# Two positions per matmul in the k transforms, copies by one engine per PSUM tile, later batches reordered, w_out sums gated, loads per batch

## The chip, the core and the metric

The kernel runs on one core of a Trainium2 chip. The metric is the device time of one execution in microseconds (us), the median of several runs. A core has TensorE (matmuls; PE, and PEld for its weight loads), VectorE (DVE), ScalarE (ACT), GpSimd (POOL) and SyncE (SP); they run side by side, each through its own queue in order, and wait for each other through semaphores. DMA engines move data between DRAM and SBUF. Matmuls write PSUM; DVE and ACT read it out.

## What is computed

Block attention with sorted blocks, then a feed-forward layer with a squared ReLU. B = 4 batches, H = 8 heads, S = 768 positions in 8 blocks of 96, D = 64; d_model = 512, d_ff = 2048.

```
P = sort_net
for _ in range(5):                       # Sinkhorn: exp, rows to 1, columns to 1
    P = exp(P - max(P)); P = P / rowsum(P); P = P / colsum(P)
k_sorted[i] = sum_j P[i, j] k_block[j]   # likewise v
attn = softmax(q_block k_sorted^T / 8) v_sorted     # block by block
x = attn as [B*S, H*D]
out = (s * relu(x w_in)**2 + b) w_out
```

Within a block the order of the 96 positions of k and v does not matter, as long as both use the same one.

## The kernel before, in words

All inputs are cast to bf16 on load, by DMAs that POOL issues. A loop of small DVE and ACT instructions computes P (L188 to L208) while TensorE runs 46 dummy matmuls (`warm_up`, L176, L522). `block_rows` and `build_pd1` / `build_pd2` spread P into matrices `pd1` (batches 0 and 1, one batch per use) and `pd2` (batches 2 and 3 together).

**k.** `kb` holds k with (head, block) on partitions: batch 0 and 2 use rows 0 to 63, batch 1 and 3 rows 64 to 127. For each of the 96 positions in a block the k transform multiplies that position's `kb` slice with P. `k_piece1` (batches 0 and 1, L272) does two matmuls per position, one for even and one for odd heads, each into half of the partitions, 32 positions to a PSUM tile `tk`; one copy takes the tile to `ks`. `k_piece2` (batches 2 and 3 together, L283) does the same with 128 rows and 16 positions to a tile. So batch 0 takes 192 matmuls and 3 tiles, batch 1 the same, batches 2 and 3 together 192 matmuls and 6 tiles.

**v.** Batch 0's v is transformed directly into `VS[0]` (`v_piece0`, L292; 24 of the 64 columns go through `vt`, a copy that ACT makes in `v_perm`, L154). The other batches' v is transformed the other way round, written to DRAM (`dv`) and read back transposed (`v_read`, L336).

**Attention and feed-forward.** Time goes in eight half batches t = 0 to 7. Per t: four `s_piece` (scores and exp), four `p_piece` (times v, normalised into `X[t]`), one `t_piece` (transposed into `XT[t]`), `ffn1` (8 steps of 8 matmuls into `hps`, ACT's ReLU to `rt`, DVE's square to `gt`), `ffn2` (3 outputs tiles of 16 matmuls `ops`, DVE adds the bias, SP stores). Batch 0's preparation stands ahead of `ffn1(0)`, which goes in two halves of 192 columns. Everything later is cut into pieces that a `Queue` hands out between the matmuls of `ffn1` and `ffn2`: a queue of N pieces and n slots runs pieces until N * at // n are done at slot `at`. The order on each engine is the program's order.

**PSUM.** Two pools, whose buffers go round in the order in which tiles are asked for: `psa` (3 buffers of 2 banks: `hps`, `tk`, `tv`, `sc`, `tq`, `tr`, `bps`) and `psb` (2 buffers of 1 bank: `ops`, `pv`, `wp`, `pe`). Other pools: `rt` 3, `gt` 2, `vn` 6, `vs` 2, `qr` 2.

**Bias.** b times the column sums of w_out: POOL adds the 16 blocks of `wo` into `csum` (L557 to L559) as soon as w_out is there; `bias_piece` (L495), in `ffn2(0)`, multiplies it with ones and DVE makes `bias`. No `ops` tile is read out before that.

**Loads.** POOL issues, in order: v of batch 0, k of batch 0 in two parts, half of q, masks, w_in, the other half of q, v of batch 1, w_out, q and k of batch 1. v of batches 2 and 3 follows after `ffn1(1)`'s pieces, k of both and q of batch 2 after `ffn2(0)`.

Of the kernel before, what the change touches and what calls it, by code (L numbers as in the profile page):

```python
# [9 lines left out]
FP = mybir.dt.float32  # L10
# [8 lines left out]
def kernel(  # L19
# [12 lines left out]
    nc = tc.nc  # L32
# [239 lines left out]
    def k_piece1(b, c0, eng):  # L272

        pr = brows(b)[1]
        ps = psa.tile([128, CQ, 32], FP, tag="a", name="tk")
        for c in range(CQ):
            for e in range(2):
                nc.tensor.matmul(out=ps[e * 64:(e + 1) * 64, c, :], lhsT=kb[pr, c0 + c, :],  # L278
                                 rhs=pd1[pr, e], start=True, stop=True)
        g0 = (b % 2) * 32  # L280
        evac(ks[:, g0:g0 + 32, c0:c0 + CQ], ps.rearrange("p c g -> p g c"), eng)

    def k_piece2(c0, eng):  # L283

        ps = psa.tile([128, 16, 64], FP, tag="a", name="tk")
        for c in range(16):
            for e in range(2):
                nc.tensor.matmul(out=ps[e * 64:(e + 1) * 64, c, :], lhsT=kb[:, c0 + c, :],
                                 rhs=pd2[:, :, e], start=True, stop=True)
        evac(ks[:, :, c0:c0 + 16], ps.rearrange("p c g -> p g c"), eng)  # L290

    def v_piece0(d0, eng):  # L292

        ps = psa.tile([128, 16, 64], FP, tag="a", name="tv")
        rhs = pd1[0:64].rearrange("p e m i -> p (e m i)")
        for t in range(16):
            if d0 + t < NV:
                nc.tensor.matmul(out=ps[0:BLK, t, :], lhsT=vt[:, d0 + t, :], rhs=rhs,
                                 start=True, stop=True)
            else:  # L300
                nc.tensor.matmul(out=ps[:, t, :], lhsT=vb[0:64, :, d0 + t], rhs=rhs,  # L301
                                 start=True, stop=True)
        evac(VS[0][:, :, d0:d0 + 16], ps[0:BLK].rearrange("p t g -> p g t"), eng)

# [238 lines left out]
    def P(t, hp, *r):  # L543
# [21 lines left out]
    qu = Queue([lambda: (q_piece(1, 0, "s"), q_piece(1, 2, "v")), nothing,
                lambda: (k_piece1(1, 0, "v"), k_piece1(1, CQ, "s"), k_piece1(1, 2 * CQ, "v")),
                bias_piece, nothing, S2(2, 0), nothing, S2(2, 2), V2[0], V2[1], V2[2], V2[3],
                P2(2, 0), V2[4], P2(2, 2), seq(V2[5], lambda: v_read(2, nc.gpsimd)), S2(3, 0),
                T(2), P2(3, 0), S2(3, 2), nothing, P2(3, 2), nothing, T(3)], 24)
# [7 lines left out]
    def K2(i):
        return lambda: [k_piece2(16 * (i + j), "vsv"[j]) for j in range(3)]

    ffn1(2)  # L580
    ffn1(3, Queue([nothing, lambda: (q_piece(2, 0, "v"), q_piece(2, 2, "v")), nothing, K2(0),
                   nothing, nothing, K2(3), nothing], 8))
# [43 lines left out]
```

## Time and profile before

| | us |
|---|---|
| median of 3 runs | 264.79 (263.52 to 265.55) |
| profiled execution | 263.0 |
| its span, first to last instruction | 261.3 |
| DVE busy in the span | 124.5 (48%) |
| ACT busy in the span | 111.4 (43%) |
| POOL busy in the span | 36.2 (14%) |

A profile is one execution, taken by the hardware. The page gives busy time per engine; the span in 40 equal slices, where a digit is the busy share in tenths and PEclk the TensorE clock that was granted, in tenths of full speed; and the DMA queues. Other views group instructions by line and form, list busy times in chosen stretches, follow the chain of work that ended last back from the end, or list instructions in order of time. "L278" is line 278. "issue" stands where an engine waited for nothing that the profile shows.

### The profile page before, as it was taken

How to read it: one execution, taken by the hardware profiler on the slowest of the kernel's cores; microseconds unless marked ns; L12 is line 12 of the kernel's file. 1: busy time of each engine (PE TensorE's matmuls, PEld its weight loads, DVE VectorE, ACT ScalarE, POOL GpSimd, SP SyncE). 2: the span in 40 equal slices, each digit the busy share in tenths (PEclk: the TensorE clock that was granted, in tenths of full speed). 3: DMA queues.
4: the chain of work that ended last, by engine and by line, in shares of the span. 5: the costliest groups of instructions: out<-in, count | busy, mean ns of one | idle time of the engine just before them, and what ended most of it. 6: DMA issues, size and time to landing. Idle time of an engine off the chain costs nothing.

```text
span 261.3 us, 5765 instructions
## 1 busy us (share of the span) xinstructions
PE 239.3 (92%) x2536; PEld 145.9 (56%) x2556; DVE 124.5 (48%) x240; ACT 111.4 (43%) x139; POOL 36.2 (14%) x47
## 2 busy tenths in 40 slices
PE   8976889769994999999988999999999999999993
PEld 2466878754572455565654555556555555664441
DVE  5623849965651334634854525444446263442221
ACT  5542436554430466376454242466442427662000
POOL 7720039940002000520000000000000000000000
PEclk9975558999995999999999999999999999999998
DMA  4999999301598999399400111200011211000122
GB/s 52 201 209 209 211 207 214 76 0 28 96 220 105 204 243 304 112 180 134 77 3 3 49 74 41 83 0 3 0 43 40 80 43 41 3 0 20 63 80 82
DMA packets 20217, 25.02 MB, mean 96 GB/s; under 512 B 7456, under 2 KB 14368, under 8 KB 19744
## 3 DMA queue, kind: packets, MB, share of 16 engines
q0 software_dynamic: 8416, 15.21, 33.7%
q1 hardware_dynamic: 11776, 9.45, 13.0%
q8 instruction: 20, 0.33, 0.6%
q14 instruction: 5, 0.04, 0.0%
HBM read 29.63 MB, written 8.65 MB: 147 GB/s over the span
## 4 chain that ended last, share of the span: by engine, by line
PE 84%; DVE 9%; issue 3%; ACT 2%; DVEq 0%
PE ops L453 32%; PE hps L427 30%; PE wp L179 5%; DVE gt L432 4%; PE tk L278 3%; PE sc L353 3%; PE pv L380 3%; PE tr L408 2%; DVE x L385 1%; PE tv L301 1%; ACT rt L431 1%; PE tq L266 1%; PE tq L251 1%; PE tv L330 1%; DVE ks L235 1%
## 5 line engine op out<-in xcount | busy, mean ns | idle before, releaser
L427 PE MATMUL hps<-xt,wi 128*128 128x384 bf16 (+1 forms) x576 | 90.0, 313 | 6.3 <-DVE ks L235 2.0
L453 PE MATMUL ops<-wo,gt 128*128 128x512 bf16 x364 | 87.5, 381 | 1.7 <-issue 0.8
L427 PEld LDWEIGHTS <-wi 128*128 128x128 bf16 x576 | 54.9, 100 | 36.3 <-issue 8.3
L431 ACT ACTIVATE rt<-hps 128x768 bf16<-128x768 f32 (+1 forms) x72 | 53.2, 739 | 43.9 <-PE hps L427 42.9
L432 DVE TENSOR_TENSOR gt<-rt 128x768 bf16<-128x768 bf16 (+1 forms) x72 | 43.5, 611 | 49.8 <-ACT rt L431 49.7
L453 PEld LDWEIGHTS <-gt 128*128 128x128 bf16 x384 | 35.6, 98 | 39.7 <-issue 1.4
L356 ACT ACTIVATE at<-sc 96x768 bf16<-96x768 f32 x32 | 24.4, 802 | 29.9 <-PE sc L353 29.9
L444 DVE SCALAR_TENSOR_TENSOR ot<-ops,s_bc,bias 128x512 f32<-128x512 f32 x24 | 18.0, 749 | 39.7 <-PE ops L453 39.6
L385 DVE TENSOR_TENSOR x<-pv,rec 96x512 bf16<-96x512 f32 (+1 forms) x36 | 22.6, 628 | 1.2
L237 ACT COPY xt<-tr 128x1536 bf16<-128x1536 bf16 x7 | 10.1, 1438 | 23.9 <-PE tr L408 23.9
L559 POOL TENSOR_TENSOR csum<-csum,wo 128x512 f32<-128x512 f32 x14 | 16.2, 1155 | 1.1
L235 DVE CAST ks<-tk 128x1024 bf16<-128x1024 f32 x8 | 9.6, 1221 | 12.0 <-PE tk L278 12.0
L380 PEld LDWEIGHTS <-at 96*128 96x128 bf16 (+1 forms) x256 | 12.4, 105 | 4.8 <-ACT at L356 1.0
L278 PE MATMUL tk<-pd,kb 64*64 64x32 bf16 x384 | 8.1, 190 | 7.1 <-issue 6.2
L380 PE MATMUL pv<-vs,at 96*128 96x66 bf16 (+1 forms) x256 | 13.0, 200 | 1.3 <-DVE rec L384 0.9
L384 DVE RECIPROCAL rec<-pv 96x8 f32<-96x8 f32 (+1 forms) x36 | 6.9, 192 | 15.1 <-PE pv L380 15.1
L179 PE MATMUL wp<-zt 128*128 128x512 bf16 x46 | 12.7, 446 | 1.3 <-DVE warm L106 1.3
L278 PEld LDWEIGHTS <-kb 64*64 64x64 bf16 x384 | 7.8, 123 | 7.8 <-issue 7.7
L353 PEld LDWEIGHTS <-ks 64*96 64x96 bf16 x256 | 8.4, 127 | 5.7 <-issue 5.7
L353 PE MATMUL sc<-qt,ks 64*96 64x96 bf16 x256 | 10.9, 219 | 0.0
L237 ACT COPY qt<-tq 128x768 bf16<-128x768 bf16 (+1 forms) x6 | 5.9, 1014 | 10.9 <-PE tq L251 8.3
L179 PEld LDWEIGHTS <-zt 128*128 128x128 bf16 x46 | 5.0, 110 | 8.5 <-issue 3.5
(70 smaller groups left out, 126.3 us busy)
## 6 DMA issues: line engine op xcount, KB each, us to landing
out_dram<-ot SPq DMA_DIRECT2D x24, 256.0 KB, 2.0
qr<-in_q_dram POOLq DMA_DIRECT2D x3, 768.0 KB, 22.2
wi<-in_moe_w_in_dram POOLq DMA_DIRECT2D x2, 1024.0 KB, 16.9
wo<-in_moe_w_out_dram POOLq DMA_DIRECT2D x2, 1024.0 KB, 28.0
vb<-in_v_dram POOLq DMA_DIRECT2D x2, 768.0 KB, 15.4
vb<-in_v_dram POOLq DMA_DIRECT2D x1, 1536.0 KB, 10.8
kb<-in_k_dram POOLq DMA_DIRECT2D x1, 1536.0 KB, 13.5
dv<-vn SPq DMA_DIRECT2D x6, 256.0 KB, 6.7
```

The source lines that it names most:

```text
L179: nc.tensor.matmul(out=wp, lhsT=zt[:, 0:128], rhs=zt, start=True, stop=True)
L278: nc.tensor.matmul(out=ps[e * 64:(e + 1) * 64, c, :], lhsT=kb[pr, c0 + c, :], rhs=pd1[pr, e], start=True, stop=True)
L353: nc.tensor.matmul(out=sc[:, e, n * BLK:(n + 1) * BLK], lhsT=ks[pr, g0 + n, :], rhs=QT[b][pr, hp, q0:q0 + BLK], start=True, stop=True)
L356: nc.scalar.activation(out=at, in_=sc[:, :, 0:TG], func=AF.Exp, scale=scale)
L380: nc.tensor.matmul(out=pv[e][0:m, (n - n0) * VW:(n - n0 + 1) * VW], lhsT=atf[:, c0:c0 + m], rhs=VS[b][:, gi, :], start=True, stop=True)
L385: nc.vector.tensor_tensor(out=x[:, n0:n0 + nn, hp * 128:(hp + 1) * 128].rearrange("p n (e d) -> p e n d", e=2), in0=pvv[:, :, :, 0:D], in1 ...
L427: nc.tensor.matmul(out=hps[:, f, 0:nt], lhsT=wi_at(hp, f0 + f), rhs=xt[:, hp, c0:c0 + nt], start=(hp == 0), stop=(hp == NHP - 1))
L431: nc.scalar.activation(out=rt[:, :, 0:nt], in_=hps[:, :, 0:nt], func=AF.Relu)
L432: nc.vector.tensor_tensor(out=gt[:, f0:f0 + 2, c0:c0 + nt], in0=rt[:, :, 0:nt], in1=rt[:, :, 0:nt], op=ALU.mult)
L444: nc.vector.scalar_tensor_tensor(out=ot, in0=ops, scalar=s_bc, in1=bias, op0=ALU.mult, op1=ALU.add)
L453: nc.tensor.matmul(out=ops, lhsT=gt[:, f, m * 128:(m + 1) * 128], rhs=wo_at(f), start=(f == 0), stop=(f == NF - 1))
L559: nc.gpsimd.tensor_tensor(out=csum, in0=csum, in1=wo_at(f), op=ALU.add)
```

## The change

- **k transforms.** One `k_piece` for all batches. A matmul takes two neighbouring positions as its 128 weight columns and even and odd heads together as its columns: 48 matmuls for batch 0, 48 for batch 1, 48 for batches 2 and 3. The result has position parity on the partition halves where `ks` has head parity, so each tile is copied in four quarters of 64 partitions, all four by one engine. The quarters of one parity are `half(0)` and `half(1)`; for batches 2 and 3 they are queued as two pieces (`K2`). Batch 0 keeps the order of positions; for later batches even positions come first in `ks`, then odd ones, and `v_read` reads v in that order, in two DMAs.
- **Batch 0.** `vt` and `v_perm` are gone; all 64 columns of `v_piece0` come from `vb`. `q_half(0)` moves into the warm-up, which has 50 matmuls of 256 columns instead of 46 of 512. k is four tiles, copied by DVE, ACT, DVE, ACT. `build_pd2` moves behind `ffn1(0)`; two score pieces of t = 1 move ahead of it, two `V1` pieces behind it; `t_piece(1)` is copied by DVE instead of ACT.
- **w_out sums.** A one-element copy on POOL from the end of `X[1]` comes before them; they are split into 7 additions before and 8 after the load of v of batch 3.
- **Loads.** Half of q first, then k, v, the rest of q; v, k and q of batch 2 are issued ahead of `ffn1(0)`; batch 3's v and k are loaded by themselves.
- **Queues.** `ffn2(0)` and `ffn2(1)` have q and k of batch 1 in five slots instead of two; k of batches 2 and 3 is spread over `ffn1(2)` and `ffn1(3)` (15 pieces, 16 slots) instead of two lumps of three tiles in `ffn1(3)`.

```diff
-    load_v(*brows(0))
-    load_k(*brows(0), 2)
-    load_q(0, slice(0, 64))
+    load_q(0, slice(0, 64))
+    load_k(*brows(0))
+    load_v(*brows(0))
+    load_q(0, slice(64, 128))
...
-            wp = psb.tile([128, 512], FP, tag="b", name="wp")
+            wp = psb.tile([128, 256], FP, tag="b", name="wp")
...
+    def k_piece(b, c0, nc2, nb, eng):
...
+        pr = brows(b)[1] if nb == 1 else slice(0, 128)
+        rhs = (pd1[pr].rearrange("p e m i -> p (e m i)") if nb == 1
+               else pd2.rearrange("p b e m i -> p (b e m i)"))
+        if nc2 * nb > 8:
+            ps = psa.tile([128, nc2, nb * 64], FP, tag="a", name="tk")
+        else:
+            ps = psb.tile([128, nc2, nb * 64], FP, tag="b", name="tk")
+        for c in range(nc2):
+            nc.tensor.matmul(out=ps[:, c, :],
+                             lhsT=kb[pr, c0 + 2 * c:c0 + 2 * c + 2, :].rearrange("p c d -> p (c d)"),
+                             rhs=rhs, start=True, stop=True)
+        g0 = (b % 2) * 32
+
+        def half(cp):
+            if b == 0:
+                cs = slice(c0 + cp, c0 + 2 * nc2, 2)
+            else:
+                cs = slice(cp * (BLK // 2) + c0 // 2, cp * (BLK // 2) + c0 // 2 + nc2)
             for e in range(2):
...
+                evac(ks[e * 64:(e + 1) * 64, g0:g0 + nb * 32, cs].rearrange(
+                         "p (b g) c -> p b g c", b=nb),
+                     ps[cp * 64:(cp + 1) * 64].rearrange(
+                         "p c (b e g) -> p e b g c", b=nb, e=2)[:, e], eng)
+
+        half(0)
+        return lambda: half(1)
...
-    warm_up(46)
+    warm_up(38)
+    q_half(0, "s")
+    warm_up(12)
     build_pd1()
-    v_perm(16, NV)
-    for i, c0 in enumerate(range(0, BLK, CQ)):
-        k_piece1(0, c0, "vsv"[i])
-    q_half(0, "s")
-    v_piece0(0, "v")
-    v_piece0(16, "v")
+    k_piece(0, 0, 16, 1, "v")()
+    k_piece(0, 32, 16, 1, "s")()
+    k_piece(0, 64, 8, 1, "v")()
+    k_piece(0, 80, 8, 1, "s")()
+    v_piece0(0, 16, "v")
+    v_piece0(16, 16, "s")
+    v_piece0(32, 16, "v")
     s_piece(0, 0)
-    v_piece0(32, "v")
     s_piece(0, 1)
-    v_piece0(48, "v")
+    v_piece0(48, 16, "v")
     s_piece(0, 2)
     s_piece(0, 3)
-    build_pd2()
+    q_half(1, "s")
     for hp in range(NHP):
         p_piece(0, hp, 0, 2)
-    q_half(1, "s")
     t_piece(0, "v", 0, 2)
+    s_piece(1, 0)
+    s_piece(1, 1)
+
+    load_v(*brows(2))
+    load_k(*brows(2))
+    load_q(2)
...
+    gate = sk.tile([1, 1], BF)
+    nc.gpsimd.tensor_copy(out=gate, in_=X[1][0:1, HB - 1, d_model - 1:d_model])
...
+    csums(0, 8)
+    ffn1(1, Queue([V1(i) for i in range(2, 6)] + [lambda: v_read(1, nc.sync)] + [nothing] * 3, 8))
+    load_v(*brows(3))
+    csums(8, NF)
...
+    def K2(c0, eng):
+        return [lambda: rest.append(k_piece(2, c0, 8, 2, eng)), lambda: rest.pop()()]
+
+    pieces = [lambda: q_piece(2, 0, "v"), lambda: q_piece(2, 2, "v")]
+    for i in range(6):
+        pieces += K2(i * 16, "sv"[i % 2])
+    qu = Queue(pieces + [nothing], 16)
+    ffn1(2, qu)
+    ffn1(3, qu)
```

## Rows read from the trace of the kernel before

**Rows 1.** The page: TensorE's busy time, its granted clock in slices, its instruction queue.
```profile
PE 239.3 (92%) x2536; PEld 145.9 (56%) x2556; DVE 124.5 (48%) x240; ACT 111.4 (43%) x139; POOL 36.2 (14%) x47
...

...
q8 instruction: 20, 0.33, 0.6%
```

**Rows 2.** Busy times in stretches: engines, then granted clock, DMA share, GB/s.
```profile
15.26:36.52 21.26, 16.77 (x410) 15.84 (x410) 10.82 (x19) 6.99 (x9) 0.56 (x2) 0.54 1.16 210
36.52:58.15 21.63, 18.05 (x232) 16.13 (x232) 17.49 (x33) 11.87 (x22) 17.32 (x15) 0.90 0.65 113
...
71.19:111.26 40.07, 35.83 (x505) 20.96 (x510) 16.78 (x29) 16.78 (x18) 5.10 (x4) 0.91 0.95 196
111.26:139.87 28.61, 26.29 (x372) 17.07 (x371) 16.57 (x23) 15.55 (x19) 1.62 (x2) 1.00 0.62 89
```

**Rows 3.** The chain that ended last, in order of time: start us, us, what.
```profile
13.99 0.37 PE pe L220 x2
...
15.26 3.79 PE tk L278 x138
19.04 2.74 issue
...
59.61 0.33 PE tv L316 x2
...
75.51 2.70 PE tk L278 x164
78.21 3.48 issue
...
82.95 1.49 PE ops L453 x3
84.44 1.24 PE bps L497 x2
...
96.36 0.54 PE pv L380 x16
...
111.42 13.02 PE hps L427 x80
```

**Rows 4.** Instructions in order of time: the Sinkhorn loop's last one on DVE.
```profile
11.73 0.21 DVE L208 TENSOR_TENSOR sn<-sn,rrec 32x64 f32<-32x64 f32 x1
```

**Rows 5.** Instructions in order of time: POOL, held until earlier loads had landed.
```profile
10.47 0.92 POOL L161 DMA_DIRECT2D wo<-in_moe_w_out_dram  x1 [0.52 <-DMA vb<-in_v_dram]
...
16.67 0.54 POOL L90 DMA_DIRECT2D kb<-in_k_dram  x1 [1.39 <-DMA qr<-in_q_dram]
```

**Rows 6.** Instructions in order of time: v transforms of batch 0.
```profile
28.35 1.37 PE L301 MATMUL tv<-pd,vb 64*128 64x64 bf16 x14
```

**Rows 7.** Groups by line and form: busy us, mean ns of one, then idle before.
```profile
L431 ACT ACTIVATE rt<-hps 128x768 bf16<-128x768 f32 x56 | 45.4, 810 | 34.4 <-PE hps L427 34.4
L432 DVE TENSOR_TENSOR gt<-rt 128x768 bf16<-128x768 bf16 x56 | 31.2, 558 | 47.2 <-ACT rt L431 47.2
...
L235 DVE CAST ks<-tk 128x1024 bf16<-128x1024 f32 x8 | 9.6, 1221 | 12.0 <-PE tk L278 12.0
...
L235 DVE COPY qt<-tq 128x1536 bf16<-128x1536 bf16 x4 | 6.9, 1754 | 2.7 <-PE tq L266 2.7
...
L235 DVE CAST vn<-tv 128x512 bf16<-128x512 f32 x6 | 4.1, 683 | 0.0
L237 ACT CAST ks<-tk 128x1024 bf16<-128x1024 f32 x4 | 4.0, 1012 | 7.0 <-PE tk L278 6.4 <-PE tk L288 0.7
```

**Rows 8.** Instructions in order of time, ffn1(0): one addition on POOL, one square on DVE.
```profile
47.86 1.15 POOL L559 TENSOR_TENSOR csum<-csum,wo 128x512 f32<-128x512 f32 x1
47.92 1.31 DVE L432 TENSOR_TENSOR gt<-rt 128x384 bf16<-128x384 bf16 x1
```

**Rows 9.** Instructions in order of time, ffn1(3): TensorE after three tk tiles.
```profile
131.67 4.06 PE L427 MATMUL hps<-xt,wi 128*128 128x384 bf16 x24 [0.99 <-DVE ks L235]
```

More of the change, by code (lines that the diff above doesn't have):

```diff
@@ L75 @@
     vb = const.tile([128, 128, D], BF)
-    NV = 24
-    vt = sk.tile([64, NV, BLK], BF)
     qr = {}
@@ L101 @@
     nc.sync.dma_start(out=b_bc, in_=moe_b.to_broadcast([128, 1]))
-    zt = const.tile([128, 512], BF)
+    zt = const.tile([128, 256], BF)
     nc.vector.memset(zt, 0.0)
@@ L270, in q_piece @@
              ps[:, :, 0:S].rearrange("q a (t p) -> q a p t", t=TQ), eng)
[L272 to L276, printed above, removed]
-            for e in range(2):
[L278 to L303, printed above, removed]
+    def k_piece(b, c0, nc2, nb, eng):
[16 more added lines that the diff above has]
+                cs = slice(cp * (BLK // 2) + c0 // 2, cp * (BLK // 2) + c0 // 2 + nc2)
+            for e in range(2):
+                evac(ks[e * 64:(e + 1) * 64, g0:g0 + nb * 32, cs].rearrange(
[4 more added lines that the diff above has]
+        return lambda: half(1)
@@ new lines, in v_piece0 @@
+    def v_piece0(d0, n, eng):
+        if n > 8:
+            ps = psa.tile([128, n, 64], FP, tag="a", name="tv")
+        else:
+            ps = psb.tile([128, n, 64], FP, tag="b", name="tv")
+        for t in range(n):
+            nc.tensor.matmul(out=ps[:, t, :], lhsT=vb[0:64, :, d0 + t],
+                             rhs=pd1[0:64].rearrange("p e m i -> p (e m i)"),
+                             start=True, stop=True)
+        evac(VS[0][:, :, d0:d0 + n], ps[0:BLK].rearrange("p t g -> p g t"), eng)
@@ L339, in v_read @@
         src = dv[1] if b == 1 else dv[2][(b - 2) * 64:(b - 1) * 64]
-        eng.dma_start(out=VS[b][:, :, 0:D], in_=src.rearrange("g c d -> c g d"))
+        for cp in range(2):
+            eng.dma_start(out=VS[b][cp * (BLK // 2):(cp + 1) * (BLK // 2), :, 0:D],
+                          in_=src.rearrange("g (c two) d -> two c g d", two=2)[cp])
     XT, AT, X = {}, {}, {}
@@ L550, in V1 @@
         return lambda: v_piece1(i * 8, "v")
-    ffn1(0, Queue([P(0, 0, 2, 2), P(0, 1, 2, 2), P(0, 2, 2, 2), P(0, 3, 2, 2), SC(1, 0),
-                   lambda: t_piece(0, "v", 2, 2), SC(1, 1), SC(1, 2)], 8), 0, 2)
-    ffn1(0, Queue([SC(1, 3), P(1, 0), nothing, P(1, 1), P(1, 2), P(1, 3), nothing, T(1)], 8), 2, 2)
-    csum = const.tile([128, d_model], FP)
-    nc.gpsimd.tensor_tensor(out=csum, in0=wo_at(0), in1=wo_at(1), op=ALU.add)
-    for f in range(2, NF):
-        nc.gpsimd.tensor_tensor(out=csum, in0=csum, in1=wo_at(f), op=ALU.add)
@@ L561 @@
-    ffn1(1, Queue([V1(i) for i in range(6)] + [lambda: v_read(1, nc.sync), nothing], 8))
-    load_v(slice(128, 256), slice(0, 128))
-    V2 = [lambda c0=c0: v_piece2(c0, "s") for c0 in range(0, BLK, 16)]
[L565 to L569, printed above, removed]
+    ffn1(0, Queue([P(0, 0, 2, 2), P(0, 1, 2, 2), P(0, 2, 2, 2), P(0, 3, 2, 2), SC(1, 2),
+                   lambda: t_piece(0, "v", 2, 2), SC(1, 3), P(1, 0)], 8), 0, 2)
@@ new lines, with csums @@
+    ffn1(0, Queue([nothing, P(1, 1), nothing, P(1, 2), nothing, P(1, 3), nothing,
+                   lambda: t_piece(1, "v")], 8), 2, 2)
+    build_pd2()
+    V1(0)()
+    V1(1)()
+    csum = const.tile([128, d_model], FP)
+    gate = sk.tile([1, 1], BF)
+    nc.gpsimd.tensor_copy(out=gate, in_=X[1][0:1, HB - 1, d_model - 1:d_model])
+    def csums(f0, f1):
+        for f in range(f0, f1):
+            if f == 1:
+                nc.gpsimd.tensor_tensor(out=csum, in0=wo_at(0), in1=wo_at(1), op=ALU.add)
+            elif f > 1:
+                nc.gpsimd.tensor_tensor(out=csum, in0=csum, in1=wo_at(f), op=ALU.add)
@@ new lines @@
+    csums(0, 8)
+    ffn1(1, Queue([V1(i) for i in range(2, 6)] + [lambda: v_read(1, nc.sync)] + [nothing] * 3, 8))
+    load_v(*brows(3))
+    csums(8, NF)
+    V2 = [lambda c0=c0: v_piece2(c0, "s") for c0 in range(0, BLK, 16)]
+    qu = Queue([lambda: q_piece(1, 0, "s"), lambda: q_piece(1, 2, "v")]
+               + [lambda c0=c0: k_piece(1, c0, 16, 1, "vsv"[c0 // 32])() for c0 in range(0, BLK, 32)]
+               + [bias_piece, S2(2, 0), V2[0], S2(2, 2), V2[1], V2[2], V2[3],
+                  P2(2, 0), V2[4], P2(2, 2), seq(V2[5], lambda: v_read(2, nc.gpsimd)), S2(3, 0),
+                  T(2), P2(3, 0), S2(3, 2), nothing, P2(3, 2), nothing, T(3)], 24)
@@ L575 @@
     load_q(3)
[L577 to L582, printed above, removed]
+    rest = []
+    def K2(c0, eng):
[6 more added lines that the diff above has]
+    ffn1(3, qu)
     qu = Queue(attn(4) + attn(5), 24)
@@ L587 @@
     ffn1(5)
-    qu = Queue([lambda: (q_piece(3, 0, "s"), q_piece(3, 2, "v")), nothing]
+    qu = Queue([lambda: q_piece(3, 0, "s"), lambda: q_piece(3, 2, "v")]
                + attn(6) + attn(7), 24)
```

10 lines of the change are left out of this document (2 added, 8 removed).

## Prediction

> **What bounds the kernel now.** I read the share of the span per engine and the clock line first, then the busy times by stage, then the chain that ended last. TensorE is busy for 92% of the span [rows 1], so a change pays only where TensorE waits or runs slowly. [...] The stages [rows 2] are: before the first k transform (to 15.26 us), the rest of batch 0's preparation (15.26 to 36.52), ffn1(0) (36.52 to 58.15), ffn1(1) (to 71.19), ffn2(0) and (1) (71.19 to 111.26), ffn1(2) and (3) (to 139.87), and 121 us that the change hardly touches. The chain [rows 3] shows two naked waits, 2.74 us at 19.04 and 3.48 us at 78.21, both inside a run of tiny `tk` matmuls, named "issue": nothing in the profile held TensorE.
>
> What are they? Counting matmuls in program order, the first wait falls after the 223rd, the second after about the 990th. Each comes with one weight load, so 767 x 2 = 1534 instructions lie between them: six blocks of 256. The instruction queue [rows 1] moved 20 packets of 0.33 MB in all: 16 KB each, which for some 5,100 TensorE instructions is 256 a packet. So TensorE had used up a block and the next had not come. The previous block ends lie 128 matmuls earlier, at about 16.3 and 76.1 us by the spacing in [rows 3], so the next block came some 5.5 us after it each time, at a DMA share near 1 [rows 2]. 128 `tk` matmuls last 2.7 us; they outrun that.
>
> [...]
>
> **The change, part by part.** All at the profiled run's 263.0 us, span 261.3.
>
> *Start.* The Sinkhorn chain ends at 11.94 [rows 4], but warm-up holds TensorE until 13.99 [rows 3]. Now 50 warm-ups have half the columns, and `q_half(0)` stands among them. Warm-up columns until about 6.7 us run at half rate as now, so 25 of the 50 are done by then; the other 25 at 0.107 us and 48 transposes (some 0.8) end near 10.3, or near 11.2 where q is late: v's 0.79 MB released POOL at 10.47 and 1.97 MB at 16.67 [rows 5], so q's 0.39 MB, now first, should land by 8.5. k (1.18 MB in all) lands near 12.5 and v near 16.7, both in time. The step from `pe` to `pd1` stays 1.27 us, so `pd1` is ready at 13.25 instead of 15.26.
>
> *Batch 0, 13.25 to ffn1(0).* k: 48 matmuls for 192. Their shape isn't in the trace. Nearest are the v transforms (64x128 weights, 64 columns) at half clock, 14 in 1.37 us or about 0.09 each [rows 6], and, below, `pv` at full clock, 16 in 0.54 us, 0.034 [rows 3]. The copies get dearer: a quarter of a tile is 64 partitions by 512. No row has 64 partitions, but on DVE 512 elements take 0.68 us and 1024 take 1.22; on ACT 1024 take 1.01 and 768 take 0.81, so 512 about 0.6 [rows 7]. A tile copied once now costs four quarters: 2.7 us on DVE, 2.4 on ACT. Bounds: half the price (if 64 partitions were cheaper) and 1.22 (if a copy cost the same whatever its size). I take 0.68 and 0.6, since rows scale with elements.
> Walk at half clock: k tiles done 17.6; DVE copies the first until 17.4 and the third (256 elements a quarter) until 19.1, ACT the second until 18.4 and the fourth until 19.9. v tiles 1 to 3 end on TensorE at 19.0, 20.5, 21.9, two scores 23.0, the last v tile, which waits for a PSUM buffer, 24.6, two scores 25.7, `q_half(1)` 27.2, four `pv` with 0.6 us of DVE each 30.0, transposes 30.8, two scores of block 1, 31.9. The clock was still full 1.2 us after `pd1` before; the same again makes it 31.3. At full clock throughout the copies would set the pace: about 28. Gain 36.5 - 31.3 = **5.2**. `build_pd2` (1.5 us on this path before) moves behind ffn1(0), where the `xt` copy covers it.
>
> *ffn1(0), 21.63 us.* In it DVE sets the pace: a `gt` that starts beside a `csum` addition of POOL ends only after it, in 1.3 us [rows 8], where one of twice the elements takes 0.56 alone [rows 7]; so 0.35 is its own. The gate moves all 15 additions behind `X[1]`. Left is TensorE: 128 matmuls of 192 columns at half of 13.02/80 = 0.163 us [rows 3], 10.5; other pieces some 4.0; the first 3.9 us at half clock as before, +1.9; then `xt` copied by DVE (1.75, as `qt` [rows 7]). 18.1, gain **3.5**.
>
> *ffn1(1).* Two of six `V1` pieces leave (0.33 each [rows 3]): gain **0.6**. But the additions now run here. A `gt` of 768 elements (0.56 [rows 7]) waits for at most one addition, 1.15, which the `vn` copy (PSUM source) can use; with `vn` some 1.3 to 1.9 a step against 1.4 to 1.7 on TensorE. I take nothing (three `rt` buffers cover it); at worst 8 x 1.15 + 4 x 0.68 + 8 x 0.56 = 16.4 against 12.4, a loss of 4. POOL's queue: behind the gate wait stand 7 additions, `load_v(3)` (which waits for `V1`), 8 more; 15 x 1.23 = 18.5 us from 46 plus the load is 66, and the bias matmul comes at about 71. Nothing waits.
>
> *Loads.* v, k and q of batch 2 are issued earlier; DMA stays full until about 60 us instead of 48. The transfers of batch 1 are ahead of them in POOL's queue; SP's `dv` writes and `v_read(1)` (two DMAs instead of one, same bytes) share the engines, but `VS[1]` is wanted only 20 us later: zero.
>
> *ffn2(0), (1), 40.07 us.* k of batch 1 goes from 7.44 us (75.51 to 82.95, the wait in it) to 48 x 0.034 = 1.6 (bounds 1.6 to 4.3); the three `ops` and the bias after it ran at half clock, 1.49 + 1.24 [rows 3], and shrink by about 1.4. DVE has four quarters twice (5.4 us), `qt`, and then the bias; `S2(2,0)` waits about 0.6 for the last. Gain **6.7**. TensorE's blocks: 128 matmuls now take 9 us or more wherever DMA is full, against 5.5.
>
> *ffn1(2), (3), 28.61 us.* Now 15 pieces in 16 slots. A `tk` tile holds one of three psa buffers over two steps; buffers go round in order (after three `tk` the next `hps` waits for the first one's copy [rows 9]), so `hps` has two. With `hps` 1.30, `tk` 8 x 0.055 (128 columns, a third of 0.163, `hps` [rows 3]) = 0.45, `rt` 0.81 [rows 7]: an ACT tile runs `rt`, two quarters, `rt`, two quarters, 3.65 to 4.0 us from one `tk` to the next, a DVE tile 4.35, TensorE alone 3.05. Four steps and `q` 7.0, 0.35 more for the first tile, 22.7 for the rest: 30.05 to 30.2. **Loss 1.6**, bounds: 25 (only TensorE) and 33. [...]
>
> Sum: 5.2 + 3.5 + 0.6 + 6.7 - 1.6 = 14.4; 263.0 - 14.4 = 248.6. The profiled run lies 1.8 under the median of 264.79; I forecast **250**, between the two.
>
> **Rivals.**
> *A. The waits stay* at the k transforms, for a reason that isn't block size: 2.7 + 3.5 + 1.4 of half clock given back, near 257. For it: they sit at k both times. Against: the block count, and 192 of these matmuls at 129 to 138 us without a wait, when DMA was quiet. 0.10.
> *B. The additions bite again:* 4 us in ffn1(1), and if each also waits for a `gt` of 0.56, 8.4 us more on POOL, so the bias comes 4 late: 258. 0.10.
> *C. Full clock in the preparation* (-3.3) and `hps` in ffn1(2), (3) not held up (-3): near 244. For it: k keeps TensorE less starved. Against: the half clock came while TensorE was densely busy with small matmuls. 0.15.
> *D. Slower: a quarter costs what a tile cost* (1.22 and 1.01). Six tiles of batches 2 and 3: 3 x 4 x (0.54 + 0.4) = 11 us on that loop; 4.5 in the preparation, 4 in ffn2(0): 250 + 20 = 270. It decides from about 1.05 us a quarter. Against: [rows 7]. 0.05.
> My forecast, 246 to 254: 0.60.
>
> **Numbers.** 250 is the forecast's. Leaving out D, half of B's upper tail and C's far end, 243 to 258. A measurement of this kernel tells about 1% (2.6 us) from no change; under 262.1 lie the forecast, A, B and C but for their tails, 0.90; 0.05 within; 0.05 above 267.4.
>
> **What would show it.** `pd1` near 13.3; no "issue" wait over 1 us in any k transform; first `hps` near 31; quarters of 0.6 to 0.7 us; `gt` of ffn1(0) near 0.35 and stretched ones in ffn1(1); the stage of ffn2(0), (1) near 33.5; in ffn1(2), (3) `tk` waiting for `ks` copies, the stage near 30. I am wrong if a new block wait appears, if quarters cost over 0.9, or if bias waits for `csum`.

## The result, and the profile after

The changed kernel takes 249.4 us (median of 4 runs, 248.36 to 252.31); the kernel before, beside it, 265.17 (263.52 to 266.09). The ratio is 0.940, 95% interval 0.933 to 0.947: faster by nearly 16 us. 250.0 was forecast, in 243 to 258. The profiled execution took 249.47, its span is 247.8. Executions more than 1.5% above the fastest of their kernel are left out of every ratio.

First the clock line of the page of before, which the prediction reads, with its DMA line (tenths, 40 slices of 6.5 us, counted from 0; digit 5 of the clock line, in slices 3 to 5 and 12, is what the prediction calls the half clock):

```profile
PEclk9975558999995999999999999999999999999998
DMA  4999999301598999399400111200011211000122
```

The same from the page of after (slices of 6.2 us), with the busy times and the instruction queue:

```profile
PE 233.1 (94%) x2128; PEld 140.9 (57%) x2128; DVE 133.2 (54%) x260; ACT 116.3 (47%) x156; POOL 39.3 (16%) x51
...
PEclk9955579999999999999999999999999999999999
DMA  5999999999799929991001212000012120001122
...
q8 instruction: 16, 0.26, 0.5%
```

The second dip of the clock, slice 12, is gone. The hole in the DMA line is gone: before, the engines stood nearly still from 48 to 60 us (DMA share 0.02); after, they work through (1.07). The loads that fill it turn out to matter a great deal. Busy times by stage, columns as in [rows 2]; the stages are those of the prediction:

```profile
13.53:31.04 17.51, 14.68 (x233) 13.46 (x232) 11.23 (x20) 10.44 (x16) 2.31 (x4) 0.50 1.10 206
31.04:49.38 18.34, 17.02 (x224) 15.36 (x223) 12.98 (x37) 10.30 (x20) 2.99 (x5) 0.93 1.22 210
49.38:61.87 12.49, 12.24 (x74) 6.48 (x73) 11.36 (x14) 5.67 (x7) 10.46 (x10) 1.00 1.12 219
61.87:97.24 35.37, 34.29 (x368) 18.42 (x366) 21.93 (x36) 18.09 (x21) 11.39 (x10) 1.00 0.86 158
97.24:125.95 28.71, 26.30 (x228) 16.73 (x226) 18.13 (x28) 20.11 (x28) 1.63 (x2) 1.00 0.59 86
```

| stage | before | predicted | after |
|---|---|---|---|
| first k transform starts at | 15.26 | 13.25 | 13.53 |
| first `hps` starts at | 36.52 | 31.3 | 31.04 |
| ffn1(0) | 21.63 | 18.1 | 18.34 |
| ffn1(1) | 13.04 | 12.4 | 12.49 |
| ffn2(0), (1) | 40.07 | 33.4 | 35.37 |
| ffn1(2), (3) | 28.61 | 30.05 to 30.2 | 28.71 |

The chain of after has something that [rows 3] did not have: DMAs. Pieces in order of time, start, us, what:

```profile
13.25 0.23 DVE pd L511
13.53 1.88 PE tk L278 x32
...
60.91 8.34 DMA dv<-vn
...
69.39 0.34 SPq L345
...
69.78 12.35 DMA vs<-dv
...
82.17 0.71 PE pv L386 x16
```

The last write of batch 1's transformed v and its read back stand between 60.9 and 82.1, and the first `pv` of t = 2 waits for the read. In the list of instructions (start, us, then the idle time before and what ended it):

```profile
82.17 0.71 PE L386 MATMUL pv<-vs,at 96*128 96x66 bf16 x16 [1.03 <-DMA vs<-dv]
```

### The profile page after: what moved, and what is told of

The parts are those of the page before. It is cut to its first block, busy times and chain, and to the rows that moved or that the text cites. A ratio compares the mean times of both kernels' runs of the same rounds, so it can differ in the third digit from the quotient of the medians.

```text
span 247.8 us, 4978 instructions
## 1 busy us (share of the span) xinstructions
PE 233.1 (94%) x2128; PEld 140.9 (57%) x2128; DVE 133.2 (54%) x260; ACT 116.3 (47%) x156; POOL 39.3 (16%) x51
## 4 chain that ended last, share of the span: by engine, by line
PE 69%; DVE 12%; DMA 9%; ACT 6%; issue 1%; SPq 0%; DVEq 0%
PE ops L459 29%; PE hps L433 27%; DMA vs<-dv 5%; PE pv L386 4%; DVE gt L438 3%; DMA dv<-vn 3%; ACT rt L437 3%; PE sc L359 3%; PE tr L414 2%; ACT ks L230 2%; PE tv L304 2%; DVE ks L228 2%; DVE qt L228 1%; PE tk L278 1%; DMA sn<-in_sort_net_dram 1%
## 5 line engine op out<-in xcount | busy, mean ns | idle before, releaser
L459 PE MATMUL ops<-wo,gt 128*128 128x512 bf16 x384 | 90.5, 380 | 0.0
L230 ACT COPY xt<-tr 128x1536 bf16<-128x1536 bf16 x6 | 8.6, 1438 | 23.6 <-PE tr L414 23.6
L228 DVE CAST ks<-tk 64x512 bf16<-64x512 f32 (+1 forms) x28 | 18.5, 662 | 1.7 <-PE tk L278 1.3
L583 POOL TENSOR_TENSOR csum<-csum,wo 128x512 f32<-128x512 f32 x14 | 17.6, 1255 | 1.0
L230 ACT CAST ks<-tk 64x512 bf16<-64x512 f32 (+1 forms) x24 | 13.9, 580 | 7.2 <-PE tk L278 6.9
L172 PE MATMUL wp<-zt 128*128 128x256 bf16 x50 | 9.6, 321 | 1.1 <-DVE warm L104 1.1
L278 PE MATMUL tk<-pd,kb 64*128 64x64 bf16 (+1 forms) x144 | 8.3, 216 | 0.9 <-DVE pd L511 0.9
L278 PEld LDWEIGHTS <-kb 64*128 64x128 bf16 (+1 forms) x144 | 7.4, 106 | 3.0 <-issue 2.2
L228 DVE COPY qt<-tq 128x1536 bf16<-128x1536 bf16 x4 | 7.0, 1754 | 3.5 <-PE tq L259 3.5
## 6 DMA issues: line engine op xcount, KB each, us to landing
wo<-in_moe_w_out_dram POOLq DMA_DIRECT2D x2, 1024.0 KB, 30.2
```

The costliest lines, as they stand in the source:

```text
L278: nc.tensor.matmul(out=ps[:, c, :], lhsT=kb[pr, c0 + 2 * c:c0 + 2 * c + 2, :].rearrange("p c d -> p (c d)"), rhs=rhs, start=True, stop=True)
L459: nc.tensor.matmul(out=ops, lhsT=gt[:, f, m * 128:(m + 1) * 128], rhs=wo_at(f), start=(f == 0), stop=(f == NF - 1))
```

## Experiments

**The two waits belong to a count of instructions.** `e1_shift`, the kernel before with its warm-up matmuls twice as many and half as wide:

```diff
-            wp = psb.tile([128, 512], FP, tag="b", name="wp")
+            wp = psb.tile([128, 256], FP, tag="b", name="wp")
...
-    warm_up(46)
+    warm_up(92)
```

> The kernel before with 92 warm-up matmuls of 256 columns instead of 46 of 512: the same warm-up time, 46 matmuls more ahead of everything. Blocks of instructions (the prediction's reading): the waits sit at a count of TensorE matmuls (223 and about 990), so they come 46 matmuls earlier in the k transforms: after about 129 of batch 0's 192 instead of 175, after about 118 of batch 1's instead of 164. The block ahead ends at the first k matmul, so the first wait is about 2.7 us again (block due some 5.5 us after that end); for batch 1 the end falls in the ops ahead of k, so the second shrinks to some 2.0. Rival (something in the k transforms themselves, a tile, a copy or a load): both waits stay after the 175th and the 164th. The time stays within 2 us of the kernel before by either.

TensorE, instructions in order of time:

```profile
18.48 2.20 PE L278 MATMUL tk<-pd,kb 64*64 64x32 bf16 x129 [0.90 <-DVE pd L505]
23.65 1.52 PE L278 MATMUL tk<-pd,kb 64*64 64x32 bf16 x50 [2.98 <-issue]
...
80.17 2.04 PE L278 MATMUL tk<-pd,kb 64*64 64x32 bf16 x118
84.23 1.94 PE L278 MATMUL tk<-pd,kb 64*64 64x32 bf16 x66 [2.02 <-issue]
```

Against [rows 3] the first wait moved from the 175th matmul of the k transforms to the 129th, by the 46 matmuls put in ahead of it, and the second from the 164th to the 118th. Nothing else in the code of the transforms had changed. So the waits stand at a fixed place in the instruction stream, and the count of the prediction holds. That a block of 256 instructions ends there is its estimate, from that count and from the 20 packets of 0.33 MB [rows 1]; no trace shows a block arrive. The time, 272.31 us in a single run, misses the expectation of at most 2 us of change: the longer warm-up alone delayed the start by 3.2 us, and what made up the rest stays open.

Why the next block would come late is not shown either. In the tiny matmuls right ahead of the two waits of before (16.30 to 19.04 and 75.50 to 78.20 us) the DMA share was 1.12 and 1.01, ahead of the one of `e11_start` below (72.8 to 75.5) 1.02. In the first wait of before it was 1.25, but 0.28 in the second, columns as in [rows 2]:

```profile
78.20:81.70 3.50, 0.02 (x4) 0.01 (x2) 0.00 (x0) 0.49 (x1) 0.00 (x0) 0.51 0.28 66
```

So busy DMA engines alone do not explain it. The waits took 2.0 to 3.6 us each (2.74 and 3.48 before, 2.98 and 2.02 here, 3.57 in `e11_start`), and 1.55 us in `e2_oldk` below.

`e11_start`, the kernel before with the new start alone:

```diff
+    load_q(0, slice(0, 64))
+    load_k(*brows(0))
     load_v(*brows(0))
-    load_k(*brows(0), 2)
-    load_q(0, slice(0, 64))
+    load_q(0, slice(64, 128))
...
-    warm_up(46)
+    warm_up(38)
+    q_half(0, "s")
+    warm_up(12)
...
-    v_perm(16, NV)
```

> The kernel before with the new start alone: half of q first, then k, v, the rest of q; the warm-up of 50 matmuls of 256 columns with q_half(0) in it; v transformed from vb without ACT's copies. Old k transforms. My theory: k starts about 1.7 earlier (13.5); 52 more matmuls and transposes stand ahead of k, so the block end that fell at the 175th k matmul falls at about the 122nd, with the end before it in the transposes, 3 us before k starts: batch 0's wait shrinks from 2.74 to 0.5 or less; batch 1's stays at 3 to 3.5, 4 matmuls earlier (at about the 160th of 192). q_half (0.8) leaves the path behind k. 258.5 to 261. Rival (the wait belongs to k's matmuls, not to a block end): waits stay, 262 to 263.5.

260.64 us, ratio 0.985 (0.975 to 0.996).

```profile
13.54 5.30 PE L277 MATMUL tk<-pd,kb 64*64 64x32 bf16 x192 [0.90 <-DVE pd L500]
...
72.80 2.71 PE L277 MATMUL tk<-pd,kb 64*64 64x32 bf16 x160
79.07 1.04 PE L277 MATMUL tk<-pd,kb 64*64 64x32 bf16 x32 [3.57 <-issue]
```

Batch 0's wait is gone without any change of its transform; by the count the earlier block end now falls ahead of the k transforms. Batch 1's moved to the 160th, as foretold. The start is worth about 4 us (1 to 7 by the interval).

**Each part of the change undone alone.** `e2_oldk`, the changed kernel with the old k transforms for all batches (and the natural order with one read, which they imply):

```diff
-    k_piece(0, 0, 16, 1, "v")()
...
+    for i, c0 in enumerate(range(0, BLK, CQ)):
+        k_piece1(0, c0, "vsv"[i])
...
-        return [lambda: rest.append(k_piece(2, c0, 8, 2, eng)), lambda: rest.pop()()]
+        return [lambda: k_piece2(c0, eng), nothing]
```

> The changed kernel with the k transforms of before: four times as many matmuls, one copy per tile, positions in their natural order and v read back in one DMA per batch; all else as changed. Blocks of instructions: the block end falls on batch 0's 123rd k matmul, but the block before it ended near 11 us, so the next one is there by about 16.7: a wait of 0 to 1 us. In ffn2(0) a block end falls early in the third tile, 3.7 us after the one before it: a wait near 2 us. Together with 192 for 48 matmuls (some 1.5 us in the preparation, 1.5 in ffn2(0), 0.5 in ffn1(2) and (3)) the time rises by 4 to 5 us to about 254. Rival (the waits went because of the load order and the other rearrangements): no wait over 0.5 us, the time rises by 2 us at most, or falls where the copies were the limit.

250.75 us, ratio 0.949 (0.942 to 0.956): 1.2 us behind the changed kernel by the times, 2.4 by the ratios, whose intervals overlap; 4 to 5 were expected. The only trace is of an execution of 255.82 us, so its row shows where the wait falls, not what it costs:

```profile
75.30 1.25 PE L271 MATMUL tk<-pd,kb 64*64 64x32 bf16 x40 [1.55 <-issue]
```

It falls after 24 matmuls of the third tile, as the count says. The miss is in what the transforms are worth: with all the rest of the change in place, little. Why so little is not shown.

`e3_nogate`, the changed kernel without the gate:

```diff
-    gate = sk.tile([1, 1], BF)
-    nc.gpsimd.tensor_copy(out=gate, in_=X[1][0:1, HB - 1, d_model - 1:d_model])
```

> The changed kernel without the gate: the additions start as soon as w_out has landed, near 38 us, beside ffn1(0). If the gate is worth what the prediction says (3.5 us less in ffn1(0), nothing lost behind it): squares of ffn1(0) stretch to 1.1 to 1.3 us again, ffn1(0) takes 2.5 to 3.5 us longer, and the whole 2 to 3 us (252). Rival (the stretch is only moved from ffn1(0) to ffn1(1), where it costs as much, through the copies of V1 and the read of v behind them): ffn1(1) and the wait for VS[1] give it back, and the whole stays within 0.7 us.

249.29 us, 0.945 (0.941 to 0.950): not to be told from the changed kernel, as the rival has it. Seven additions ran from 36.9 to 45.4, ffn1(0) became 19.8 us long instead of 18.3, and three `hps` waited 0.46 to 0.64 us for DVE. Then ffn1(1) was quicker (12.2), the read of `VS[1]` was issued 1.8 us earlier, and the wait of 1.03 was gone. What ffn1(0) loses (1.5) is given back by the read's path (1.0), by ffn1(1) (0.3) and by a start 0.5 us earlier in this execution.

`e5_oneread`, the changed kernel with batch 1 in the natural order and one read:

```diff
-            if b == 0:
+            if b < 2:
                 cs = slice(c0 + cp, c0 + 2 * nc2, 2)
...
+        if b == 1:
+            eng.dma_start(out=VS[b][:, :, 0:D], in_=src.rearrange("g c d -> c g d"))
+            return
```

> The changed kernel with batch 1 in the natural order of positions, so that VS[1] is read by one DMA instead of two halves. In the changed kernel the read took 12.35 us from its issue, before 8.2, and TensorE waited 1.0 us for it. If the split makes the read slow: about 8 us, no wait for VS[1], the whole 1 us shorter (248.4). Rival (the read is late and slow because of what else the DMA engines carry then, the loads of batches 2 and 3): still 11 to 12 us, the wait stays within 0.3 of 1.0, the same time.

249.79 us, 0.948 (0.941 to 0.955): the same. The single read, issued at 68.28, took 13.5 us, so the split is not what made it slow. The `pv` of t = 2 starts without a wait at 82.17. But in the profiled execution the clock rose later, ffn1(0) took 19.3 us, and ffn1(2) begins at 97.24 as in the changed kernel; a gain of 1 us could not be shown.

**Each part alone, on the kernel before.** `e10_gateonly`, gate and split of the additions:

```diff
-    for f in range(2, NF):
-        nc.gpsimd.tensor_tensor(out=csum, in0=csum, in1=wo_at(f), op=ALU.add)
...
+    nc.gpsimd.tensor_copy(out=gate, in_=X[1][0:1, HB - 1, d_model - 1:d_model])
...
+    csums(0, 8)
...
     load_v(slice(128, 256), slice(0, 128))
+    csums(8, NF)
```

> The kernel before with the w_out sums gated behind X[1] and split around the load of v, nothing else. The prediction's step: gt in ffn1(0) at 0.35 instead of 1.31, so ffn1(0) about 2 to 3 shorter; six V1 steps in ffn1(1) then meet the additions, gt there 1.4 to 1.9, ffn1(1) 0 to 1 longer: 261 to 262.5. Rival (as undoing the gate in the changed kernel showed no change): 264 to 265, what ffn1(0) gains comes back in ffn1(1) or in a later bias.

262.02 us, 0.992 (0.988 to 0.996), as expected: ffn1(0) 19.5 us instead of 21.6, ffn1(1) 13.0 as before.

`e9_newk`, the new k transforms alone:

```diff
-        k_piece1(0, c0, "vsv"[i])
+        k_piece(0, c0, 16, 1, "vsv"[i])()
...
-        return lambda: [k_piece2(16 * (i + j), "vsv"[j]) for j in range(3)]
+        return lambda: [k_piece(2, 16 * (i + j), 8, 2, "vsv"[j])() for j in range(3)]
```

> The kernel before with the new k transforms alone: two positions per matmul, four quarter copies per tile by one engine, in the old order, same lumps, natural order of positions. My theory (TensorE outran its instruction blocks in the 192 tiny matmuls): block ends stay at the 95th, 223rd, ... matmul; with 144 matmuls fewer in batch 0 the 223rd lies in the v transforms, which are slower, and batch 1's k falls between two ends, so both waits of 2.74 and 3.48 us are gone. Batch 0: first hps 2 to 3.5 earlier (two tiles of four quarters on DVE take back some). ffn2(0), (1): 5 to 6.5 shorter. ffn1(3): lumps of three tiles whose copies cost 2.7 and 2.4 us instead of 1.2 and 1.0, 2 to 4 longer. In all 255 to 259. Rival (the k transform is worth what undoing it in the changed kernel cost, 1 to 1.5 us): 262 to 264, and waits stay at k.

267.36 us, 1.010 (1.005 to 1.015): slower than before, against both theories. Both waits in the k transforms are gone, the first `hps` starts at 33.90 (before 36.52), and batch 1's k transforms end 8 us earlier than before. Then the chain has:

```profile
68.68 10.18 DMA dv<-vn
...
79.01 16.51 DMA vs<-dv
```

and, on TensorE and on POOL in order of time:

```profile
95.57 1.11 PE L389 MATMUL pv<-vs,at 96*128 96x66 bf16 x16 [6.30 <-DMA vs<-dv]
...
75.12 0.54 POOL L90 DMA_DIRECT2D kb<-in_k_dram  x1 [7.52 <-PE tk L285]
```

The same rows in the kernel before, with the line of its DMA view that gives the time to landing (us, last):

```profile
82.92 0.54 POOL L90 DMA_DIRECT2D kb<-in_k_dram  x1 [13.12 <-PE tk L278]
...
80.43 0.34 SPq L340 DMA_DIRECT2D vs<-dv  x1
...
96.20 0.70 PE L380 MATMUL pv<-vs,at 96*128 96x66 bf16 x16
...
vs<-dv SPq DMA_DIRECT2D x1, 768.0 KB, 8.2
```

Before, the read of `VS[1]` (0.77 MB) is issued at 80.4 and lands 8.2 us later; k of batches 2 and 3 (1.5 MB) is issued 2.5 us after it, because it overwrites `kb` and waits for batch 1's transforms; q of batch 2 (0.75 MB) follows right behind. Faster transforms release both loads from 75.1 on, ahead of the read, and the read takes 16.5 us. The `pv` that needs it starts at 95.57 instead of 96.20: of 8 us on TensorE, 0.6 are left. And the wait leaves something behind it, columns as in [rows 2]:

```profile
95.57:99.60 4.03, 4.00 (x23) 2.06 (x25) 1.69 (x4) 0.32 (x1) 0.00 (x0) 0.53 1.00 381
```

The granted clock was 0.53 in these 4 us, where it was 1.00 before (96.20 to 100.20); the first four `ops` of them took 1.90 us instead of 1.03, and from the first `pv` to the second it takes 4.48 us instead of 2.69. So ffn1(2) begins 1.15 us later than before, and ffn1(3), where three tiles of four quarter copies come in one lump, adds 2.3.

`e12_newkloads`, the same with the loads per batch:

```diff
+    load_v(*brows(2))
+    load_k(*brows(2))
+    load_q(2)
...
-    load_v(slice(128, 256), slice(0, 128))
+    load_v(*brows(3))
...
-    load_k(slice(128, 256), slice(0, 128))
-    load_q(2)
+    load_k(*brows(3))
```

> The kernel before with the new k transforms and the loads per batch: v, k and q of batch 2 ahead of ffn1(0), v and k of batch 3 by themselves; all else as before. Theory: the 6.3 us wait for VS[1] that the new k transforms alone ran into shrinks to 0 to 2, since only half as many bytes stand ahead of the dv writes and beside the read: 258 to 261, so two parts of which one alone loses bring 3 to 6 us together. Rival (the read is late for another reason, as the DMA writes of dv themselves): still 264 to 268.

259.47 us, 0.981 (0.973 to 0.988), in the range of the theory. The read is issued at 72.65, takes 11.4 us, and `pv` starts without a wait at 86.85; ffn1(2) begins at 101.9, 9.4 us earlier than before. In ffn1(3) the lumps remain:

```profile
123.50 5.74 PE L436 MATMUL hps<-xt,wi 128*128 128x384 bf16 x24 [2.30 <-ACT ks L237]
...
133.03 1.46 PE L436 MATMUL hps<-xt,wi 128*128 128x384 bf16 x8 [2.29 <-ACT ks L237]
```

They waited 0.99 before [rows 9]; from ffn1(2)'s start to the second of these rows it takes 31.1 us instead of 27.1. In `e9_newk`, with the same two waits and the clock at 1.00, it takes 29.4; here the clock was 0.68 from 124.0 to 129.4, behind the first wait, and the 24 `hps` there took 5.74 us instead of 4.06. So in lumps the new transforms lose 2.3 us or more; spreading the pieces over sixteen slots should take that back, but no run has the spread alone.

**Loads late, in the changed kernel.** `e8_lateloads` moves only the loads of batch 2:

```diff
-    load_v(*brows(2))
-    load_k(*brows(2))
-    load_q(2)
...
+    load_v(*brows(2))
     load_v(*brows(3))
...
     ffn2(0, qu)
+    load_k(*brows(2))
     load_k(*brows(3))
+    load_q(2)
```

> The changed kernel with batch 2's loads late: v of batch 2 with that of batch 3 behind V1, k and q of batch 2 with k of batch 3 behind the k transforms of batch 1. Theory (from the trace of the new k transforms alone, where the k load followed the earlier k transforms at 75.1 us and the read of VS[1], issued at 79.0, took 16.5 us to land instead of 8.2): the early loads per batch are what lets the k gain through. Here 1.5 MB of v stand ahead of the dv writes and 1.5 MB of k beside the read, so VS[1] lands 3 to 6 us later than 83 and the first pv of t = 2 waits 3 to 6 us: 252 to 255. Rival (the early loads are what crowds the DMA, and the 1.0 us wait for VS[1] goes): 248 to 249.

257.78 us, 0.976 (0.971 to 0.981): 8.4 us more than the changed kernel, beyond the upper end of what the theory said, far from the rival. The chain, and TensorE at its end:

```profile
60.08 9.78 DMA dv<-vn
...
70.39 17.65 DMA vs<-dv
...
88.09 1.12 PE L386 MATMUL pv<-vs,at 96*128 96x66 bf16 x16 [7.16 <-DMA vs<-dv]
```

Up to there this kernel runs like the changed one; the read takes 17.65 us instead of 12.35, the `pv` waits 7.16 us, 6.1 more than in the changed kernel, and in the 3.9 us behind it the granted clock was 0.56 (four `ops` in 1.90 us instead of 1.03): from the first `pv` to the second it takes 4.34 us instead of 2.71. Three moved loads cost more than half of the change's gain. Which of v, k and q does it was not separated.

**The clock in the preparation.** `e7_busier`, the changed kernel with dummy matmuls between batch 0's pieces:

```diff
-    warm_up(12)
+    warm_up(16)
     build_pd1()
...
+    for _ in range(8):
+        nc.tensor.matmul(out=wq, lhsT=zt[:, 0:128], rhs=zt, start=True, stop=True)
...
+        for _ in range(4):
+            nc.tensor.matmul(out=ps[:, 0:4, :], lhsT=zt[:, 0:128], rhs=zt, start=True, stop=True)
```

> The changed kernel with TensorE kept busy by dummy matmuls in batch 0's preparation: 16 instead of 12 warm-ups at the end, 8 of 256 columns behind the spreading of pd1, 4 ahead of each v tile, 2 ahead of each score pair of batch 0. No output changes. Theory (the half clock from about 13.4 to 32.7 us follows on TensorE standing idle for copies and loads): the clock stays full, the dummies cost 0.1 us each where TensorE waits anyway, first hps at 28.5 to 30 instead of 31.0, ffn1(0) begins at full clock (2 us): 245.5 to 248. Rival (the level does not depend on this, or the work between is too little): half clock as before and the dummies cost 0 to 2: 249 to 251.5.

252.78 us, 0.956 (0.949 to 0.963): theory and rival both missed. Stretches, columns as in [rows 2], and two v tiles in order of time:

```profile
16.20:17.80 1.60, 1.55 (x16) 1.52 (x16) 1.54 (x4) 1.56 (x3) 0.54 (x1) 1.00 1.25 213
...
20.00:21.00 1.00, 1.00 (x5) 0.47 (x6) 0.10 (x1) 0.96 (x1) 0.00 (x0) 0.50 1.17 221
...
24.60:28.00 3.40, 3.40 (x30) 2.45 (x30) 0.74 (x1) 0.81 (x1) 0.48 (x1) 0.50 1.21 238
```

```profile
16.25 1.63 PE L306 MATMUL tv<-pd,vb 64*128 64x64 bf16 x16 [0.78 <-DMA vb<-in_v_dram]
...
20.90 1.63 PE L306 MATMUL tv<-pd,vb 64*128 64x64 bf16 x16
```

The half clock came between 18.4 and 20 us instead of at 13.5, and stayed until 34.6 to 37, though TensorE stood still for less than 1 us between 12.4 and 28. Long idle stretches are not what brings it here: the one wait of size, 0.78 us, ended at 16.25, over 2 us ahead of the fall. What does stays open. The dummies moved the first `hps` to 34.67. And a v tile takes 1.63 us at full clock and at half, with PEld busy 95% of the first stretch, which points to the weight loads as its limit (an estimate from these rows, not tested). Rival C's full clock would have given these tiles nothing.

**A version made of the better parts.** `e13_mix`, the changed kernel with the natural order, one read per `VS`, and batches 2 and 3 transformed as before:

```diff
-            if b == 0:
+            if b < 2:
...
-        return [lambda: rest.append(k_piece(2, c0, 8, 2, eng)), lambda: rest.pop()()]
+        return [lambda: k_piece2(c0, eng), nothing]
...
-        for cp in range(2):
...
+        eng.dma_start(out=VS[b][:, :, 0:D], in_=src.rearrange("g c d -> c g d"))
```

> The changed kernel with the natural order and one read for VS, and batches 2 and 3 transformed as before (two matmuls per position, one copy per tile), in the changed kernel's slots. From the traces: no wait for VS[1] (1.0), and ffn1(2), (3) at 24.8 to the last pair of hps as with the old k transforms instead of 26.1, no wait of S2(4,0) (0.4): 1.5 to 2.5 less than the changed kernel, 246.5 to 248.5. Rival (32 matmuls per two steps outrun the instruction blocks again, or the gains are taken back at the next wait): 249 to 251.

247.42 us (247.22 to 248.65, 6 runs), 0.938 (0.934 to 0.942). In ffn1(3):

```profile
110.57 0.69 PE L302 MATMUL tk<-pd,kb 128*64 128x64 bf16 x32
111.20 2.77 PE L440 MATMUL hps<-xt,wi 128*128 128x384 bf16 x16
113.90 0.70 PE L302 MATMUL tk<-pd,kb 128*64 128x64 bf16 x32
```

Two steps take 3.33 us and no `hps` of this loop waits; the changed kernel takes 3.5 to 3.66. The DMA share was 0.42 from 104.5 to 121 us, and no "issue" wait shows there. It is about 2 us faster than the changed kernel by the medians; the intervals of the two ratios, from different comparisons, overlap. `e14_mixnogate` is the same without the gate (the two lines of `e3_nogate`):

> The same mixture without the gate, so that seven additions run beside ffn1(0). From the trace without the gate: ffn1(0) 1.5 longer, ffn1(1) and the way to VS[1] as much shorter or, with the VS[1] wait already gone, nothing given back: 0 to 1.5 slower than the mixture with the gate. Rival: 0.5 faster.

248.38 us, 0.941 (0.937 to 0.945): about 1 us slower by the medians, with intervals that overlap. The first `pv` of t = 2 does not wait with the gate or without it, so here nothing gives the longer ffn1(0) back.

## Why the prediction came out right, and where it did not

The time came out 0.6 us from the forecast, but not each term did. Set against the table, the start was 0.3 us better than the sum had it, ffn1(0) 0.2 and ffn1(1) 0.1 worse, ffn2(0), (1) 2.0 worse, ffn1(2), (3) 1.4 better. Two terms missed in opposite directions and nearly cancel; that the total came so close is partly luck.

*Waits as block ends: the count is right,* the block itself stays an estimate. No "issue" wait of half a microsecond is left at the k transforms; the queue moved 16 packets of 0.26 MB instead of 20; `e1_shift` and `e11_start` moved the waits by the number of matmuls put in. Rival A falls. But the prediction tied the end of the waits to the fewer matmuls, and `e11_start` and `e2_oldk` show that in batch 0 the new start does it too, with 192 matmuls. It is not just any shift: in `e1_shift`, which by the count puts the earlier block end at the first k matmul, a wait of 2.98 us stayed. And "a DMA share near 1" is the stage's: in the second wait itself it was 0.28.

*Start: right,* 13.53 against 13.25.

*Batch 0: right in sum.* Quarters, by group:

```profile
L228 DVE CAST ks<-tk 64x512 bf16<-64x512 f32 x24 | 16.7, 697 | 1.7 <-PE tk L278 1.3
...
L230 ACT CAST ks<-tk 64x512 bf16<-64x512 f32 x20 | 12.2, 612 | 7.1 <-PE tk L278 6.9
```

0.70 and 0.61 us, where 0.68 and 0.6 were taken: on DVE half the partitions save nothing, and rival D falls. The `xt` copy on DVE was 0.95 us, not 1.75.

*csum: right in ffn1(0), and rival B falls.* Additions ran beside ffn1(1), `gt` there took up to 1.91 us, `vn` (out of PSUM) 0.68 us beside them as without them, and the stage is 12.49 long.

*Loads at zero, "VS[1] is wanted only 20 us later": the step that failed.* The prediction looked at how late the read is wanted and not at what releases the k load beside it. Undoing batch 2's early loads costs 8.4 us (`e8_lateloads`), and without them and the spread pieces the k transforms, which the prediction credited with most of the 6.7 us of ffn2(0), (1), make the kernel slower (`e9_newk`); put back in the changed kernel, the old transforms cost only 1.2 to 2.4 (`e2_oldk`). The number held because the change brings the loads along. The chain of [rows 3] could not warn of it, since in the kernel before TensorE came to the `pv` about 7.5 us after the read had landed; that slack, 96.2 against 80.4 + 8.2, was there to be read in the list of instructions.

*ffn2(0), (1), a gain of 6.7: mis-sized, 4.7 came.* 1.0 of the difference is the new wait for `VS[1]`. For k, 5.8 was taken and about 5.1 came: the 7.44 us hold 0.33 of an `ops` whose record is missing from the trace (the program has four ahead of the bias, the trace three), and the new k tiles cost 2.0 us from 65.38 to 70.00, with 12 `ops` of 0.216 taken off, instead of 1.6. The first scores took 0.78 us instead of 0.49, and each further slot lengthens the `ops` around it by about 0.1 (four in 0.97 us ahead of `tq`, in 0.86 ahead of `tv`). Against that, the wait of 0.6 for the last copy did not come.

*ffn1(2), (3), a loss of 1.6: mis-sized.* 0.1 was measured. The prediction took [rows 9], and the text ahead of it says, that PSUM buffers go round in the order of asking. TensorE after, in order of time, and one row of ACT:

```profile
104.47 0.61 PE L278 MATMUL tk<-pd,kb 128*128 128x128 bf16 x8
105.36 2.76 PE L433 MATMUL hps<-xt,wi 128*128 128x384 bf16 x16 [0.29 <-DVE qt L228]
107.70 1.17 ACT L230 CAST ks<-tk 64x512 bf16<-64x512 f32 x2
107.96 0.61 PE L278 MATMUL tk<-pd,kb 128*128 128x128 bf16 x8
108.92 2.76 PE L433 MATMUL hps<-xt,wi 128*128 128x384 bf16 x16 [0.35 <-ACT ks L230]
111.52 0.61 PE L278 MATMUL tk<-pd,kb 128*128 128x128 bf16 x8
112.58 2.76 PE L433 MATMUL hps<-xt,wi 128*128 128x384 bf16 x16 [0.45 <-ACT rt L437]
```

A new `tk` starts every 3.5 to 3.66 us, where 3.65 to 4.35 were worked out, and at 107.96 while the last tile's second half is still being copied (until 108.87): here the new tile did not get the buffer of the tile three requests back. Waits of 0.3 to 0.45 us per pair of steps are what is left. `e13_mix`, with one copy per tile instead of four, has none of them, and its stage takes 27.6 us instead of 28.7; so the work that empties PSUM limits this loop, by about 1 us.

*What the parts are worth together.* On the kernel before, the start gives 4 us, the gate 2, the k transforms with the loads 5: 11 of the 16, if they simply add. The other order of batch 0's pieces and the spread pieces of ffn1(2), (3) were not tried alone, nor the early loads without the transforms.

## What to carry to other kernels

Before crediting a faster engine with its time, look for what its last read releases: here a 1.5 MB load that waited for the k transforms moved ahead of a smaller read (0.77 MB) on which the next stage hangs, and with copies that came in lumps the gain became a loss. Ask of every transfer costed at nothing how much slack its consumer had before and how much is left once all the other gains are taken. Price a long wait of TensorE with what follows it: here waits of 6.3 (`e9_newk`) and 7.2 us (`e8_lateloads`) were followed by about 4 us at a granted clock of 0.53 and 0.56, which cost 1.6 to 1.8 us more. And when a wait with no cause in the profile moves with the number of instructions ahead of it, count instructions before blaming the code at which it shows.

## What was not expected of the hardware

- A DMA read of 0.77 MB took 8.2 us from issue to landing when it was issued 2.5 us ahead of a 1.5 MB load (before). It took 11.4 (`e12_newkloads`) to 13.6 us (`e13_mix`) in one piece, and 12.35 for the later half of two (the changed kernel), when a load of 0.75 MB was issued 0.2 to 2.9 us behind it, 16.5 us with loads of 1.5 and 0.75 MB issued 3.9 and 3.4 us ahead of it (`e9_newk`), and 17.65 us for its later half with 0.75 MB ahead of it and 1.5 MB around it (`e8_lateloads`).
- The k transforms of batch 0 ran at a granted clock of 1.00 in some executions (48 in 1.56 us, `e3_nogate`) and of 0.50 in others (2.72 us, the changed kernel); in `e7_busier` a v tile took 1.63 us at either.
- Half the partitions did not make this copy out of PSUM cheaper: 64x512 took 0.70 us on DVE (the changed kernel), 128x512 took 0.68 [rows 7].
- `gt` of 768 elements took 0.56 us alone [rows 7] and up to 1.91 us beside additions on POOL (the changed kernel, at 57.28).
